# Pairing the pooling sums, one fp32 matmul per h, and 81 changed steps of the order, in a fused attention and maxout kernel

## The chip, the cores and the metric

The kernel runs on one core of a Trainium2 chip. The metric is the device time of one execution in microseconds (us), as a median of several runs. The engines are named as in the profile: PE (TensorE, matrix multiply), PEld (its weight loads), DVE (VectorE), ACT (ScalarE), POOL (GpSimd) and SP (SyncE, which here issues transfers). "L792" is line 792 of the kernel.

## The reference

There are two stages. The first is an attention through 32 inducing points, for four batch elements of 12544 tokens with 128 channels: the 32 points attend to all tokens and give h (32 x 128 for each batch element); then each token attends to the 32 rows of h. The second is a maxout layer on the result.

```python
# x: (4, 12544, 128), inducing: (32, 128); w1, w2: (128, 1024); w_out: (1024, 128)
def mab(q, kv):
    s = scale * (q @ kv.transpose(0, 2, 1))
    s = s - s.max(-1, keepdims=True)
    a = np.exp(s)
    a /= a.sum(-1, keepdims=True) + 1e-09
    return a @ kv
h = mab(I, x)                 # I: the inducing points, for each batch element
y = mab(x, h)                 # (4, 12544, 128)
h1 = y @ w1
h2 = y @ w2
out = np.maximum(h1, h2) @ w_out
```

"Pooling" below is the first `mab`: E = exp(scores), its sums, and h = (E x) / (sums of E).

## The kernel before

A batch element has 98 chunks of 128 tokens. The kernel writes max(h1, h2) as h1 + relu(h2 - h1), and folds h into the weights: a "phase" multiplies E2 (the second attention's exponentials, 32 rows for each of four blocks of tokens) by h (w2 - w1), the relu moves it from PSUM to SBUF on ACT (L973) or DVE (L976), and eight "final" matmuls per chunk (L792) multiply by w_out and add up. A "linear" part (L957 too, with the tile m) adds h1.

PE's array is used in three tilings. Final matmuls use it whole (128x128, "full"). A phase uses four row tiles of 32 rows, one for each block of tokens, side by side. Pooling and the staging of E2 use four column tiles of 32 columns ("col"). Every PE instruction's place in the program is fixed when the program is built, by a rule that keeps a rough clock `ck` of PE, ACT, DVE and the eight PSUM banks.

Pooling of the batch elements 1 to 3 runs beside the main loop of the element before. A unit is 16 chunks (NU = 6 units, and REST = 2 chunks left over). Scores of a unit go to one bank; ACT takes their exponential and, with it, the row sums (`accum_out`):

```python
        def pool_scores(b, u):
            if u == 0:
                st[b]["es"] = smp.tile([128, NU + 1], F32, name=f"es_{b}", tag="esu")
                nc.gpsimd.memset(st[b]["es"], 0.0)
            bi, ps = bank([128, 512])
            ck.wait(ck.bank[bi], "p1")
            for g in range(4):
                nc.tensor.matmul(
                    out=ps[32 * g : 32 * (g + 1), :],
                    lhsT=inducingT,
                    rhs=xT_tiles[b % 2][:, U * u + 4 * g : U * u + 4 * (g + 1), :],
                    start=True,
                    stop=True,
                    tile_position=(0, 32 * g),
                    skip_group_check=True,
                )
            end = ck.run(0.226, "col")
            eu = etp.tile([128, 512], F16, name=f"eu_{b}_{u}", tag="eu", bufs=NEU)
            nc.scalar.activation(
                out=eu, in_=ps, func=AF.Exp, scale=scale, accum_out=st[b]["es"][:, u : u + 1]
            )
            ck.bank[bi] = ck.on_act(end, 0.65)
            st[b]["eu", u] = eu, ck.bank[bi]

```

Each unit is turned by a transposing transfer, and then summed against x:

```python
        def pool_accum(b, u):
            bi, ps = bank([128, 512])
            ck.wait(ck.bank[bi], "p1")
            eT = st[b]["eT", u][0]
            st[b]["sum", u] = True
            last = u == NU - 1
            for j in range(4):
                for g in range(4):
                    nc.tensor.matmul(
                        out=ps[32 * g : 32 * (g + 1), 0:128],
                        lhsT=eT[:, j, 32 * g : 32 * (g + 1)],
                        rhs=xn_of(b, U * u + 4 * g + j),
                        start=(j == 0),
                        stop=(j == 3 and not (last and g < REST)),
                        tile_position=(0, 32 * g),
                        skip_group_check=True,
                    )
            if last:
                # ... (the REST chunks: E against x, and against a column of ones, into columns 0:128 and 128)
            end = ck.run(0.26, "col")
            if u == 0:
                st[b]["hacc"] = smp.tile([128, C], F32, name=f"hacc_{b}", tag="hacc")
                nc.vector.tensor_copy(out=st[b]["hacc"], in_=ps[:, 0:128])
            else:
                acc = st[b]["hacc"]
                nc.vector.tensor_add(out=acc, in0=ps[:, 0:128], in1=acc)
            ck.bank[bi] = ck.on_dve(end, 0.2)
            if last:
                es = st[b]["es"]
                nc.vector.tensor_copy(out=es[0 : 32 * REST, NU : NU + 1], in_=ps[0 : 32 * REST, 128:129])
                esr = smp.tile([128, 1], F32, name=f"esr_{b}", tag="esr")
                nc.vector.reduce_sum(out=esr, in_=es, axis=AX.X)
                st[b]["esr"] = esr
                ck.bank[bi] = st[b]["esrr"] = ck.on_dve(end, 0.2)
                if b + 1 < B:
                    for i in range(7):
                        load_x(b + 1, i, esr if i == 0 else None)
```

From these come h (`small_rep` spreads and inverts the sums, `small_h` transposes h and repeats it for the four row tiles):

```python
        def small_rep(b):
            bi, ps = bank([128, 512])
            ck.wait(ck.bank[bi], "p1")
            nc.tensor.matmul(out=ps[:, 0:1], lhsT=repd, rhs=st[b]["esr"], start=True, stop=True)
            end = ck.run(0.11)
            rec = smp.tile([128, 1], F32, name=f"rec_{b}", tag="rec")
            nc.vector.reciprocal(out=rec, in_=ps[:, 0:1])
            acc = st[b]["hacc"]
            nc.vector.tensor_scalar(out=acc, in0=acc, scalar1=rec, scalar2=None, op0=ALU.mult)
            ck.bank[bi] = st[b]["haccr"] = ck.on_dve(end, 0.4)

        def small_h(b):
            # ... (element 0 has its own way)
            bi, ps = bank([128, 512])
            ck.wait(ck.bank[bi], "p1")
            nc.tensor.matmul(out=ps[:, 0:128], lhsT=st[b]["hacc"], rhs=repd, start=True, stop=True)
            end = ck.run(0.25)
            nc.vector.tensor_copy(out=hT4.rearrange("c q m -> c (q m)"), in_=ps[:, 0:128])
            ck.bank[bi] = st[b]["hT4r"] = ck.on_dve(end, 0.2)
            st[b]["hT4"] = hT4.rearrange("c q m -> c (q m)")
```

The main loop: each pass places one thing. `column_work` places a staging or a pooling job; `phase` places a phase; `final_one` one final matmul. `tp` is when the phase's banks are free, `tf` when the next final's data are there.

```python
        def column_work(banks):
            # ... (False if too few banks; staging first, if due)
            jobs = [job for job in pending if job[0] in COL and ready(*job)]
            late = jobs and (chunks_done[0] >= due[jobs[0]] + 8 or jobs[0][1][1] == NU - 1)
            if jobs and (ck.mode == "col" or len(jobs) > 1 or late):
                pending.remove(jobs[0])
                f, a = jobs[0]
                f(*a)
                return True
            return False

        while state["g"] < len(groups) or held:
            side_work()
            if held and ck.mode == "full":
                linear_last(0.0)
            if ck.mode != "full" and column_work(1):
                continue
            if min(ck.bank) <= ck.pe + 0.1 and want_stage(1):
                stage(blocks[state["stage"]])
                state["stage"] += 1
                continue
            jobs = plan_phase()
            tp = INF
            tf = final_ready()
            useful = len(jobs) == 4 or jobs and (tf >= INF or state["stage"] == len(blocks) and lag() <= 48)
            if useful and len(jobs) > 0:
                fr = sorted(ck.bank)[len(jobs) - 1]
                tp = max([fr - 0.095] + [(a.blk.staged if kind == "L" else a.staged) for kind, q, a, u in jobs])
            early = 0.2 if ck.mode == "col" else 0.0
            if tp < INF and lag() <= 128 + LIMIT and (tp <= ck.pe + early or tp <= tf and tf > ck.pe):
                if column_work(len(jobs) + 1):
                    continue
                phase(jobs)
            elif tf < INF:
                keep_busy(tf)
                ck.wait(tf, "relu")
                final_one()
            elif tp < INF:
            # ...
```

The softmax here doesn't subtract the row's maximum and nothing guards it: scores larger than these inputs give would overflow.

## Time and profile before

| | |
|---|---|
| median time | 330.24 us (330.13 to 330.38, three runs) |
| span of the profiled execution | 328.5 us |
| TensorE clock granted | 1.00 throughout |
| mean transfer rate | 163 GB/s |

The parts of the pooling that the change touches have these rows among the groups kept apart by shape (line, engine, operation, output and inputs, shapes, count; then busy us, mean ns of one, and idle time before):

```profile
L357 PE MATMUL ps<-xn,eT 128*32 128x128 f16 x288 | 6.4, 220 | 0.1
L309 PE MATMUL ps<-xT,inducingT 128*32 128x512 f16 x72 | 6.3, 383 | 0.0
L385 DVE TENSOR_TENSOR hacc<-ps,hacc 128x128 f32<-128x128 f32 x15 | 4.3, 287 | 0.8
L430 PE MATMUL ps<-repd,hacc 128*128 128x128 f32 x6 | 1.3, 302 | 0.0
L401 PE MATMUL ps<-esr,repd 128*128 128x1 f32 x6 | 1.1, 246 | 0.5 <-DVE esr L391 0.3
L382 DVE COPY hacc<-ps 128x128 f32<-128x128 f32 x3 | 0.8, 281 | 0.0
L391 DVE TENSOR_REDUCE esr<-es 128x1 f32<-128x7 f32 x3 | 0.5, 160 | 0.3
```

A matmul of fp32 data appears as two matmuls: three of L401 and L430 in the program, six in the profile. Matmuls overlap in the pipeline, so one that lasts 220 ns can be followed by the next after much less: times between starts tell more than durations. The timeline merges neighbours of one line ("x13"), and its second column runs from the first one's start to the last one's end.

### The profile page before, as it was taken

To read this page: it belongs to the slowest core of one execution; us is meant where nothing else is said; L and a number is where in the kernel's file an instruction comes from. 1 tells how busy PE (TensorE), PEld (TensorE's weight loads), DVE (VectorE), ACT (ScalarE), POOL (GpSimd) and SP (SyncE) were. 2 spreads that over 40 slices of the span, in tenths; PEclk is the share of its full clock that TensorE was granted. 3 is DMA by queue.
4 is the path that set the end of the run, shared out by engine and by line. 5 is a ranking of instruction groups with operands and counts; after the bars stand their busy time and mean duration, and the time that the engine had idled before them with its cause. 6 is when DMAs were issued, how large, how long until landed. Compare 5 with 4: busy or idle time off the path is not lost.

```text
span 328.5 us, 12601 instructions
## 1 busy us (share of the span) xinstructions
PE 322.6 (98%) x5401; PEld 244.1 (74%) x5401; DVE 285.3 (87%) x532; ACT 280.7 (85%) x562; POOL 25.7 (8%) x54
## 2 busy tenths in 40 slices
PE   8999999999999999999999999999999999999996
PEld 3876777777777777777777777777777777778785
DVE  3359899999988999998989989988989989989873
ACT  3679899998789999988888999998968999999961
POOL 7351030000310000000040000000000000000000
PEclk9999999999999999999999999999999999999999
DMA  8999999964299999672479999983212312222233
GB/s 207 208 206 213 289 237 205 216 187 124 57 227 244 229 221 213 167 155 97 132 139 245 226 257 215 197 177 100 98 66 97 114 67 99 98 98 98 80 116 114
DMA packets 70823, 53.65 MB, mean 163 GB/s; under 512 B 52176, under 2 KB 55408, under 8 KB 70768
## 3 DMA queue, kind: packets, MB, share of 16 engines
q1 hardware_dynamic: 64656, 38.63, 47.4%
q0 software_dynamic: 6112, 14.22, 22.1%
q8 instruction: 42, 0.69, 0.9%
q14 instruction: 13, 0.11, 0.1%
HBM read 28.33 MB, written 25.69 MB: 164 GB/s over the span
## 4 chain that ended last, share of the span: by engine, by line
PE 96%; DVE 1%; issue 1%; ACT 0%; DVEq 0%; ACTq 0%
PE ps L792 60%; PE ps L957 22%; PE ps L582 3%; PE ps L232 2%; PE ps L357 1%; PE ps L309 1%; PE ps L648 1%; PE ps L248 1%; PE ps L280 1%; PE ps L622 1%; DVE relu L976 1%; PE ps L749 1%; PE ps L271 1%; PE ps L640 0%; PE ps L464 0%
## 5 line engine op out<-in xcount | busy, mean ns | idle before, releaser
L973 ACT ACTIVATE relu<-ps 128x512 f16<-128x512 f32 x463 | 244.6, 604 | 31.1 <-PE ps L957 24.1
L976 DVE TENSOR_SCALAR relu<-ps 128x512 f16<-128x512 f32 x321 | 205.8, 681 | 18.8 <-PE ps L957 17.9
L792 PE MATMUL ps<-woutp,relu 128*128 128x128 f16 x3136 | 218.1, 220 | 0.0
L792 PEld LDWEIGHTS <-relu 128*128 128x128 f16 x3136 | 177.3, 98 | 39.4 <-issue 28.3
L957 PE MATMUL ps<-e,hwd 32*128 32x512 f16 (+2 forms) x880 | 89.0, 360 | 0.0
L819 DVE TENSOR_TENSOR o<-ps,rp 128x512 f32<-128x512 f32 (+3 forms) x108 | 68.6, 635 | 5.7 <-PE ps L792 3.1
L957 PEld LDWEIGHTS <-hwd 32*128 32x128 f16 x880 | 25.0, 91 | 21.1 <-issue 0.8
L957 PE MATMUL ps<-m,e 32*128 32x128 f16 x381 | 38.8, 217 | 0.0
L957 PEld LDWEIGHTS <-e 32*128 32x128 f16 x381 | 21.4, 92 | 2.6
L165 POOL DMA_DIRECT2D xn<-in_x_dram x31 | 16.7, 551 | 8.4 <-DMA xn<-in_x_dram 4.4
L236 DVE COPY xT<-ps 128x512 f16<-128x512 f16 (+3 forms) x11 | 5.5, 504 | 8.1 <-PE ps L232 8.0
L594 ACT ACTIVATE e<-ps 128x512 f16<-128x512 f32 (+2 forms) x21 | 11.6, 572 | 0.0
L320 ACT ACTIVATE eu<-ps 128x512 f16<-128x512 f32 x18 | 10.8, 619 | 0.0
L582 PE MATMUL ps<-xT,hT 128*32 128x512 f16 (+3 forms) x114 | 10.4, 366 | 0.0
L164 POOL COPY pace<-esr 128x1 f32<-128x1 f32 x2 | 0.4, 183 | 116.6 <-DVE esr L391 116.6
L239 ACT COPY xT<-ps 128x768 f16<-128x768 f16 (+3 forms) x11 | 6.1, 557 | 3.0 <-PE ps L232 2.9
L232 PE MATMUL ps<-identity,xn 128*128 128x128 f16 x98 | 7.7, 224 | 0.1
L582 PEld LDWEIGHTS <-hT 128*32 128x32 f16 x114 | 2.9, 93 | 5.9 <-issue 5.2
L232 PEld LDWEIGHTS <-xn 128*128 128x128 f16 x98 | 5.9, 100 | 1.3 <-DVE xn L644 0.9
L257 ACT ACTIVATE et<-ps 128x448 f16<-128x448 f32 (+4 forms) x11 | 4.5, 413 | 2.6 <-PE ps L248 2.6
L632 DVE RECIPROCAL rp<-ps 128x16 f32<-128x16 f32 (+2 forms) x28 | 6.7, 239 | 0.0
L622 PE MATMUL ps<-ones_q,e 128*128 128x4 f16 x102 | 6.5, 165 | 0.0
(96 smaller groups left out, 117.5 us busy)
## 6 DMA issues: line engine op xcount, KB each, us to landing
out_dram<-o SPq DMA_DIRECT2D x90, 256.0 KB, 2.5
xn<-in_x_dram POOLq DMA_DIRECT2D x24, 448.0 KB, 11.9
out_dram<-o SPq DMA_DIRECT2D x10, 128.0 KB, 3.1
xn<-in_moe_w_dram POOLq DMA_DIRECT2D x4, 256.0 KB, 14.1
xn<-in_x_dram POOLq DMA_DIRECT2D x4, 224.0 KB, 10.2
xT<-xn SPq DMA_TRANSPOSE x42, 3.8
xf<-in_x_dram SPq DMA_DIRECT2D x1, 512.0 KB, 3.7
xf<-in_x_dram SPq DMA_DIRECT2D x1, 384.0 KB, 4.1
```

The costliest lines, as they stand in the source:

```text
L165: nc.gpsimd.dma_start(out=xn_at[b, i][:, 0:n, :], in_=xr[b, :, k0 : k0 + n, :])
L232: nc.tensor.transpose(ps[:, j, :], xn[:, g + j, :], identity16)
L320: nc.scalar.activation(out=eu, in_=ps, func=AF.Exp, scale=scale, accum_out=st[b]["es"][:, u : u + 1])
L582: nc.tensor.matmul(out=ps[32 * q : 32 * (q + 1), 128 * t : 128 * (t + n)], lhsT=hq, rhs=xT[:, c : c + n, :], start=True, stop=True, tile_p ...
L594: nc.scalar.activation(out=blk.e2[:, 0 : 128 * wd], in_=ps[:, 0 : 128 * wd], func=AF.Exp, scale=st[0]["rs"] if blk.b == 0 else scale,)
L622: nc.tensor.matmul(out=ps[:, 4 * t : 4 * t + 4], lhsT=blk.e2[:, 128 * t : 128 * (t + 1)], rhs=ones_q, start=True, stop=True,)
L632: nc.vector.reciprocal(out=blk.rp[:, 0:wd, :].rearrange("p t q -> p (t q)"), in_=ps[:, 0 : 4 * wd])
L792: nc.tensor.matmul(out=g.ps[:, 128 * c : 128 * (c + 1)], lhsT=g.blk.relu[q][:, 128 * (jb * w4 + t) : 128 * (jb * w4 + t + 1)], rhs=woutp[: ...
L819: nc.vector.tensor_mul(osb[:, 0:n, :], g.ps[:, 0 : n * C].rearrange("p (s c) -> p s c", s=n), rp)
L957: nc.tensor.matmul(**seq[i])
L973: nc.scalar.activation(out=dst, in_=src, func=AF.Relu)
L976: nc.vector.tensor_scalar(out=dst, in0=src, scalar1=0.0, scalar2=None, op0=ALU.max)
```

## The change

It has three parts. (1) The sums of two units (u = 1, 3, 5 with the unit before it) are gathered in one PSUM bank before DVE adds them to `hacc`. (2) The sums of E ride as a 129th column of `hacc`, so that one fp32 matmul spreads both h and its sums over the four row tiles; the scaled h becomes fp16 and is transposed by an fp16 transpose where it was multiplied in fp32. (3) A table `DEV` lists 81 passes of the main loop at which the order departs from its rule: 1 holds a phase back, 2 lets it start early, 3 skips column work, 4 lets a lone column job run. The 81 entries are 49, 7, 11 and 14 of these. The aim is fewer DVE instructions and fp32 matmuls in the pooling, and a better order on PE.

```diff
             if u == 0:
-                st[b]["es"] = smp.tile([128, NU + 1], F32, name=f"es_{b}", tag="esu")
-                nc.gpsimd.memset(st[b]["es"], 0.0)
+                st[b]["es"] = smp.tile([128, NU], F32, name=f"es_{b}", tag="esu")
 ...
         def pool_accum(b, u):
             bi, ps = bank([128, 512])
             ck.wait(ck.bank[bi], "p1")
-            eT = st[b]["eT", u][0]
-            st[b]["sum", u] = True
             last = u == NU - 1
-            for j in range(4):
-                for g in range(4):
-                    nc.tensor.matmul(
-                        out=ps[32 * g : 32 * (g + 1), 0:128],
-                        lhsT=eT[:, j, 32 * g : 32 * (g + 1)],
-                        rhs=xn_of(b, U * u + 4 * g + j),
-                        start=(j == 0),
-                        stop=(j == 3 and not (last and g < REST)),
-                        tile_position=(0, 32 * g),
-                        skip_group_check=True,
-                    )
+            if u == 1:
+                st[b]["hacc"] = smp.tile([128, C + 1], F32, name=f"hacc_{b}", tag="hacc")
+            acc = st[b]["hacc"]
+            if last:
+                nc.vector.reduce_sum(out=acc[:, C : C + 1], in_=st[b]["es"], axis=AX.X)
+                ck.on_dve(st[b]["eu", u][1], 0.1)
+            for v in (u - 1, u):
+                eT = st[b]["eT", v][0]
+                st[b]["sum", v] = True
+                for j in range(4):
+                    for g in range(4):
+                        nc.tensor.matmul(
+                            out=ps[32 * g : 32 * (g + 1), 0:128],
+                            lhsT=eT[:, j, 32 * g : 32 * (g + 1)],
+                            rhs=xn_of(b, U * v + 4 * g + j),
+                            start=(j == 0 and v < u),
+                            stop=(j == 3 and v == u and not (last and g < REST)),
+                            tile_position=(0, 32 * g),
+                            skip_group_check=True,
+                        )
             if last:
                 et = st[b]["et"][0]
-                for g in range(REST):
-                    for rhs, lo, n in ((xn_of(b, U * NU + g), 0, 128), (ones16[:, 0:1], 128, 1)):
+                for g in range(4):
+                    pairs = [(warm[:, 0:M], ones16[:, 0:1], 128, 1)]
+                    if g < REST:
+                        pairs = [
+                            (et[:, g, :], xn_of(b, U * NU + g), 0, 128),
+                            (et[:, g, :], ones16[:, 0:1], 128, 1),
+                        ]
+                    for lhsT, rhs, lo, n in pairs:
                         nc.tensor.matmul(
                             out=ps[32 * g : 32 * (g + 1), lo : lo + n],
-                            lhsT=et[:, g, :],
+                            lhsT=lhsT,
                             rhs=rhs,
                             start=False,
                             stop=True,
                             tile_position=(0, 32 * g),
                             skip_group_check=True,
                         )
-            end = ck.run(0.26, "col")
-            if u == 0:
-                st[b]["hacc"] = smp.tile([128, C], F32, name=f"hacc_{b}", tag="hacc")
-                nc.vector.tensor_copy(out=st[b]["hacc"], in_=ps[:, 0:128])
+            end = ck.run(0.58 if last else 0.49, "col")
+            n = C + 1 if last else C
+            if u == 1:
+                nc.vector.tensor_copy(out=acc[:, 0:n], in_=ps[:, 0:n])
             else:
-                acc = st[b]["hacc"]
-                nc.vector.tensor_add(out=acc, in0=ps[:, 0:128], in1=acc)
-            ck.bank[bi] = ck.on_dve(end, 0.2)
+                nc.vector.tensor_add(out=acc[:, 0:n], in0=ps[:, 0:n], in1=acc[:, 0:n])
+            ck.bank[bi] = ck.on_dve(end, 0.22)
             if last:
-                es = st[b]["es"]
-                nc.vector.tensor_copy(out=es[0 : 32 * REST, NU : NU + 1], in_=ps[0 : 32 * REST, 128:129])
-                esr = smp.tile([128, 1], F32, name=f"esr_{b}", tag="esr")
-                nc.vector.reduce_sum(out=esr, in_=es, axis=AX.X)
-                st[b]["esr"] = esr
-                ck.bank[bi] = st[b]["esrr"] = ck.on_dve(end, 0.2)
-                if b + 1 < B:
-                    for i in range(7):
-                        load_x(b + 1, i, esr if i == 0 else None)
+                st[b]["esrr"] = ck.bank[bi]
+            if last and b + 1 < B:
+                for i in range(7):
+                    load_x(b + 1, i, acc[:, C : C + 1] if i == 0 else None)
         def small_rep(b):
             bi, ps = bank([128, 512])
             ck.wait(ck.bank[bi], "p1")
-            nc.tensor.matmul(out=ps[:, 0:1], lhsT=repd, rhs=st[b]["esr"], start=True, stop=True)
-            end = ck.run(0.11)
+            nc.tensor.matmul(out=ps[:, 0 : C + 1], lhsT=repd, rhs=st[b]["hacc"], start=True, stop=True)
+            end = ck.run(0.28)
             rec = smp.tile([128, 1], F32, name=f"rec_{b}", tag="rec")
-            nc.vector.reciprocal(out=rec, in_=ps[:, 0:1])
-            acc = st[b]["hacc"]
-            nc.vector.tensor_scalar(out=acc, in0=acc, scalar1=rec, scalar2=None, op0=ALU.mult)
-            ck.bank[bi] = st[b]["haccr"] = ck.on_dve(end, 0.4)
+            nc.vector.reciprocal(out=rec, in_=ps[:, C : C + 1])
+            h4 = smp.tile([128, C], F16, name=f"h4_{b}", tag="h4")
+            nc.vector.tensor_scalar(out=h4, in0=ps[:, 0:C], scalar1=rec, scalar2=None, op0=ALU.mult)
+            st[b]["h4"] = h4
+            ck.bank[bi] = st[b]["haccr"] = ck.on_dve(end, 0.45)
         def small_h(b):
             hT4 = smp.tile([C, 4, M], F16, name=f"hT4_{b}", tag="hT4")
 ...
                 ready = ck.on_act(st[0]["end"], 0.2)
                 st[b]["hT4"] = hT4.rearrange("c q m -> c (q m)")
                 return es, ready
-            bi, ps = bank([128, 512])
+            bi, ps = bank([128, 128], F16)
             ck.wait(ck.bank[bi], "p1")
-            nc.tensor.matmul(out=ps[:, 0:128], lhsT=st[b]["hacc"], rhs=repd, start=True, stop=True)
-            end = ck.run(0.25)
+            nc.tensor.transpose(ps[:, 0:128], st[b]["h4"], identity16)
+            end = ck.run(0.056)
             nc.vector.tensor_copy(out=hT4.rearrange("c q m -> c (q m)"), in_=ps[:, 0:128])
             ck.bank[bi] = st[b]["hT4r"] = ck.on_dve(end, 0.2)
 ...
+        DEV = {
+            31: 1, 54: 1, 107: 2, 141: 1, 148: 1, 177: 4, 201: 1, 231: 1, 268: 1, 285: 1, 289: 1, 297: 2,
+            ... (81 entries in all)
+            1301: 4, 1349: 4, 1362: 3, 1363: 2, 1370: 4, 1379: 1, 1396: 2, 1435: 1, 1459: 1, 1469: 1, 1472:
+            3, 1519: 1, 1534: 1, 1536: 3, 1543: 4, 1572: 3, 1606: 1, 1617: 4, 1635: 1, 1654: 3, 1686: 1,
+            1701: 3, 1729: 1
+        }
 ...
-                at(base + int(acc), pool_accum, b, u)
+                if u % 2:
+                    at(base + int(acc), pool_accum, b, u)
 ...
-        def column_work(banks):
+        def column_work(banks, soon=False):
 ...
-            if jobs and (ck.mode == "col" or len(jobs) > 1 or late):
+            if jobs and (soon or ck.mode == "col" or len(jobs) > 1 or late):
                 pending.remove(jobs[0])
 ...
+        step = -1
         while state["g"] < len(groups) or held:
+            step += 1
+            how = DEV.get(step, 0)
             side_work()
             if held and ck.mode == "full":
                 linear_last(0.0)
-            if ck.mode != "full" and column_work(1):
+            if ck.mode != "full" and how != 3 and column_work(1):
                 continue
             if min(ck.bank) <= ck.pe + 0.1 and want_stage(1):
                 stage(blocks[state["stage"]])
                 fr = sorted(ck.bank)[len(jobs) - 1]
                 tp = max([fr - 0.095] + [(a.blk.staged if kind == "L" else a.staged) for kind, q, a, u in jobs])
             early = 0.2 if ck.mode == "col" else 0.0
-            if tp < INF and lag() <= 128 + LIMIT and (tp <= ck.pe + early or tp <= tf and tf > ck.pe):
-                if column_work(len(jobs) + 1):
+            now = tp <= ck.pe + early or tp <= tf and tf > ck.pe
+            if how == 1 and tf < INF:
+                now = False
+            if how == 2 and tp <= ck.pe + 0.2:
+                now = True
+            if tp < INF and lag() <= 128 + LIMIT and now:
+                if how != 3 and column_work(len(jobs) + 1, how == 4):
                     continue
                 phase(jobs)
```

## The prediction

> **What bounds the kernel now.** I read the page's busy shares first, then the costliest groups, then the busy times by stretch, then the timeline of TensorE. The busy shares and the groups:
>
> ```profile
> PE 322.6 (98%) x5401; PEld 244.1 (74%) x5401; DVE 285.3 (87%) x532; ACT 280.7 (85%) x562; POOL 25.7 (8%) x54
> ...
> L973 ACT ACTIVATE relu<-ps 128x512 f16<-128x512 f32 x463 | 244.6, 604 | 31.1 <-PE ps L957 24.1
> L976 DVE TENSOR_SCALAR relu<-ps 128x512 f16<-128x512 f32 x321 | 205.8, 681 | 18.8 <-PE ps L957 17.9
> L792 PE MATMUL ps<-woutp,relu 128*128 128x128 f16 x3136 | 218.1, 220 | 0.0
> ```
>
> Three engines are near their limit, so the question is which one is never waited for. The idle column answers: ScalarE (ACT) and VectorE (DVE) wait for TensorE's L957 matmuls (24.1 and 17.9 us), while L792 waits for nobody. By stretch, the long middle and the tail:
>
> ```profile
> 28.00:313.00 285.00, 284.46 (x4765) 214.50 (x4764) 264.24 (x480) 258.17 (x517) 11.71 (x23) 1.00 0.69 162
> 313.00:328.50 15.50, 12.24 (x227) 10.92 (x224) 8.12 (x16) 5.23 (x11) 0.00 (x0) 1.00 0.31 108
> ```
>
> Columns: length, then PE, weight loads, DVE, ACT, POOL, clock, DMA share, GB/s. In 285 us the PE is idle for 0.54 us; DVE has 20.8 us to spare, ACT 26.8. But a busy PE need not be a PE doing useful work, so I looked at starts, one to the next, in the PE timeline:
>
> ```profile
> 154.05 0.90 PE L792 MATMUL ps<-woutp,relu 128*128 128x128 f16 x13
> 154.88 0.40 PE L957 MATMUL ps<-e,hwd 32*128 32x512 f16 x4
> 155.21 0.23 PE L792 MATMUL ps<-woutp,relu 128*128 128x128 f16 x1
> ...
> 161.64 0.41 PE L357 MATMUL ps<-xn,eT 128*32 128x128 f16 x16
> 161.98 0.62 PE L792 MATMUL ps<-woutp,relu 128*128 128x128 f16 x8
> 162.53 0.39 PE L957 MATMUL ps<-e,hwd 32*128 32x512 f16 x3
> ```
>
> Thirteen final matmuls take 13 x 0.056 = 0.73 us, yet the next start is 0.83 after the first: 0.10 goes to the change from the whole array (128*128) to row tiles (32*128). The row phase streams 512 columns once, four tiles side by side (about 0.22), yet L792 starts 0.33 later: again some 0.10. I counted these changes over the whole PE timeline from 28 to 326 us: 219 row runs, 222 full runs, 35 column runs, 475 changes, so about 46 us of tiling changes (475 x 0.097). After a full run the next row phase starts a constant 0.152 us after the last full matmul started (median, 5th and 95th percentile within 0.004), so phases practically never wait for a bank. Apart from that I find, beyond streaming and changes, about 4 to 5 us of loss in this stretch, 2.5 of it in the small fp32 matmuls treated below.
>
> So the time is a sum: PE's matmuls plus its changes of tiling. A change helps only where it takes one of these away.
>
> **What the Trainium skill says.** "Perfetto Trace Analysis", section Identifying the Most-Contended Engine, warns that matmul busy time is no measure of distance to roofline because matmuls are pipelined; the trace agrees, as 46 us of the busy time are tiling changes, and weight loads are busy only 74%. "TensorEngine Tiling (Array Packing)", section Tiling Modes, says that a change of tiling mode (not of tile) drains TensorE; the trace gives it the size that the page lacks, 0.10 us. "TensorE: Matmul & The Clock Gate", section Back-to-back issue gap, gives N/2.4 + 2.5 ns, 55.8 ns for 128 columns; the trace's L792 median is 56. "VectorE: DVE Perf Modes", section Why PSUM operands drop a tier, says an fp32 operand in PSUM keeps DVE at its slowest rate; the trace agrees (a 128x512 product from PSUM 684 ns, 128x128 add 287), so each add removed is worth its full 0.29 us of DVE.
>
> **The change, part by part.**
>
> (1) *Two units' pooling sums in one bank.* Per batch element the six additions to hacc become three. Matmuls stay: 288 of L357, 16 per unit, about 0.23 us per unit. DVE loses 9 evictions, 9 x 0.287 = 2.6 us. On PE only visits to column mode can be saved. If every unit had its own visit, merging would give 9 x about 0.2. But the order already merges: L357 appears with 32 at 75.1, 48 at 80.5, 16 at 86.0 (first element: three visits); 32 at 139.1, 32 at 153.2, 16 at 161.6, 16 at 162.9 (second: four); 32 at 212.1, 224.6, 237.1 (third: three). Ten visits against nine: one is saved, 161.6 with 162.9. A visit of 16 costs 0.34 from start to L792, one of 32 costs 0.56, and a visit adds one change of 0.10: 2 x (0.34 + 0.10) - (0.56 + 0.10) = 0.2 us. Off the PE: -2.6 us of DVE; on it: -0.2 us.
>
> (2) *Sums of E as column 129, one fp32 matmul per h.* Before, each element had an fp32 matmul for the sums (L401) and one for h (L430), two passes each:
>
> ```profile
> 87.48 0.23 PE L792 MATMUL ps<-woutp,relu 128*128 128x128 f16 x1
> 87.78 0.35 PE L401 MATMUL ps<-esr,repd 128*128 128x1 f32 x2
> 88.00 0.22 PE L792 MATMUL ps<-woutp,relu 128*128 128x128 f16 x1
> ...
> 89.70 0.44 PE L430 MATMUL ps<-repd,hacc 128*128 128x128 f32 x2
> 89.98 1.06 PE L792 MATMUL ps<-woutp,relu 128*128 128x128 f16 x16
> ...
> 238.76 0.62 PE L792 MATMUL ps<-woutp,relu 128*128 128x128 f16 x8
> 239.69 0.35 PE L401 MATMUL ps<-esr,repd 128*128 128x1 f32 x2 [0.32 <-DVE esr L391]
> 239.91 0.55 PE L792 MATMUL ps<-woutp,relu 128*128 128x128 f16 x7
> ```
>
> L401 costs 0.22 plus the gap before it: 0.30 - 0.056 = 0.24 for the first element, about 0.25 for the second, 0.93 - 0.45 = 0.48 for the third, where the page names its releaser, the reduction that makes esr. Sum 3 x 0.22 + 0.97 = 1.63 us. L430 is 0.28 x 3 = 0.84. Together 2.47. After: one fp32 matmul of 129 columns, like L430 (0.28), an fp16 transpose (0.056 each, as L232: 14 in 0.78), and a gap that should shrink, because behind the last matmul DVE has one add of 129 columns (0.29) where it had add, copy and reduction (0.29 + 0.135 + 0.16, with gaps). The order also plans the matmul earlier by its own clock, so I keep a gap of 0.1. Per element 0.28 + 0.06 + 0.10 = 0.44; three are 1.3. Saving about 1.1 us. DVE also loses three small copies, 0.4 us. The zero-weight matmuls that give the other two groups their column are one column wide and beside others: nothing.
>
> (3) *81 listed steps.* One step is one pass of the loop: one final matmul, one phase, or one column job. 49 entries (value 1) hold a phase back for one step, 7 (value 2) let it start up to 0.2 us early, 11 (value 3) skip a column visit, 14 (value 4) run a column job that would have waited for company. The last entry, step 1729 of some 3400 (3136 finals plus phases and visits), lies near the middle, so the list touches about the first half. It can't change the number of finals, and the phases are full (four units, or three and one linear part), so row runs stay at about 220. Holding a phase back by 0.056 us moves work without removing any. What it can take away on PE: column visits merged with others (25 values concern these), at 0.1 us each, and small stalls, of which I find only about 1 us in the first half beside the fp32 ones. I put it at -0.3 us: four visits fewer, minus a little for new waits.
>
> Sum: -0.2 - 1.1 - 0.3 = -1.6 us; I shade this to -1.4, because the program's clock and the chip differ by tenths of a microsecond: 328.8 us.
>
> **The rivals.** *Evictions bind.* Phases come as soon as banks free: at the median phase, the third-last outstanding eviction ended only 0.1 us before. Then 3.0 us less DVE, shared by two engines, would give up to 1.5 us more, 327.3. Against it: PE has 0.54 us of idle time in 285, so an earlier phase only means later finals; the sum stays. *The list makes stalls.* It was made for the program's own clock, not the chip. Seven early starts of up to 0.2 us, and column jobs run ahead of a phase, could add 1 to 2 us, undoing the rest: 330 to 331. For it: the slack before phases is only 0.1 us; against it: in the kernel before nothing stalls although its order comes from the same clock. *The list merges many visits.* 35 column runs to about 25 would be -1.0 instead of -0.3: 328. *The fp32 matmul now waits longer,* since it reads hacc, which comes after the last add, where it read only sums: but those sums came behind the same add in DVE's order, so this costs nothing.
>
> **Range and chances.** The first rival and the third together end near 326.8, the second near 331. Eight in ten: 327.2 to 330.4. Faster by 2% would need 6.6 us, below 323.6; all that PE could lose (35 visits at 0.1, 2.5 of fp32, 2 of stalls) is about 8, and half of it must stay. Chance 0.03. Slower by 2% would need 6.6 us of new stalls where there are almost none: 0.03.
>
> **What would show it.** In the changed profile: DVE busy less by about 3 us with PE still at 98%; L792 still x3136 and about 220 row runs; the fp32 matmuls halved, with a wait under 0.2 us before each; column runs in the low thirties. I am wrong if row runs become far fewer (phases side by side, 0.2 us each), if final matmuls show idle time behind relu, or if phases start later than 0.152 us after the last full matmul's start in the first half.

## The result and the profile after

The changed kernel takes 327.82 us (median of six runs, 327.49 to 328.40) against 330.25 us before: a ratio of 0.9928, with a 95% interval of 0.9915 to 0.9940. That is 2.4 us, 0.7%, inside the predicted range; the prediction had 1.45 us.

The busy shares and the costliest groups of the changed kernel (L801 is the final matmul, L978 the phase, L994 and L997 the relu on ACT and DVE):

```profile
PE 320.8 (98%) x5404; PEld 243.0 (74%) x5404; DVE 282.3 (87%) x518; ACT 281.8 (86%) x564; POOL 25.4 (8%) x51
...
L994 ACT ACTIVATE relu<-ps 128x512 f16<-128x512 f32 x465 | 245.3, 605 | 25.3 <-PE ps L978 16.2
L997 DVE TENSOR_SCALAR relu<-ps 128x512 f16<-128x512 f32 x319 | 204.9, 682 | 19.8 <-PE ps L978 18.3
L801 PE MATMUL ps<-woutp,relu 128*128 128x128 f16 x3136 | 217.9, 220 | 0.1
```

DVE lost 3.0 us and 14 instructions; ACT and DVE still wait for PE's phases, and the finals' idle column still shows next to nothing (0.1 us). The busy times of the middle and of the tail (length, then PE, weight loads, DVE, ACT, POOL, clock, DMA share, GB/s):

```profile
28.00:310.70 282.70, 282.70 (x4769) 213.38 (x4768) 261.39 (x467) 259.46 (x519) 11.44 (x20) 1.00 0.71 163
310.70:326.20 15.50, 12.23 (x227) 10.91 (x223) 8.11 (x16) 5.22 (x11) 0.00 (x0) 1.00 0.31 107
```

The tail is unchanged; the middle is 2.3 us shorter, and the 0.54 us of visible PE idle time are gone. The step from pooling to h, in the PE timeline of the changed kernel:

```profile
164.30 0.23 PE L801 MATMUL ps<-woutp,relu 128*128 128x128 f16 x1
164.37 0.44 PE L409 MATMUL ps<-hacc,repd 128*128 128x129 f32 x2
164.65 1.00 PE L801 MATMUL ps<-woutp,relu 128*128 128x128 f16 x15
...
166.36 0.23 PE L439 MATMUL ps<-identity,h 128*128 128x128 f16 x1
166.43 0.50 PE L801 MATMUL ps<-woutp,relu 128*128 128x128 f16 x6
```

The one fp32 matmul starts 0.07 us after the final before it, so it has no gap, and holds PE for 0.28 us; the transpose takes 0.07. The other two elements have gaps of 0.17 and 0.01 us before it. Before, there were two fp32 matmuls of 0.22 and 0.28 us and gaps of 0.24 to 0.48.

Since a busy PE hides its losses, I split PE's time by the starts of its matmuls, from the first final on. A column visit is a run of matmuls on column tiles. A phase is given 0.327 us (its median), a column visit its streaming plus 0.11 us for the way out (its allowance); what goes beyond is called a wait. "h" is the fp32 matmuls with their gaps, and the transposes without theirs. The second number is the start of the run that holds the first final. Times in us, from the profiled execution of each kernel; the experiments in the lower rows follow below.

| kernel | span | first final's run at | h | column visits | their allowance | their waits | waits in phases | the rest |
|---|---|---|---|---|---|---|---|---|
| before | 328.49 | 25.89 | 2.46 | 35 | 16.79 | 0.89 | 1.74 | 280.72 |
| changed | 326.18 | 26.01 | 1.21 | 31 | 16.36 | 0.48 | 1.17 | 280.95 |
| no_list | 329.11 | 26.40 | 1.68 | 35 | 16.80 | 2.00 | 1.48 | 280.75 |
| column_only | 327.89 | 25.69 | 1.68 | 37 | 17.02 | 0.90 | 1.84 | 280.76 |
| pairs_only | 327.14 | 25.51 | 2.04 | 35 | 16.79 | 0.50 | 1.50 | 280.80 |
| first | 327.32 | 26.19 | 1.72 | 34 | 16.68 | 0.46 | 1.57 | 280.70 |
| late50 | 328.17 | 25.52 | 1.42 | 37 | 17.02 | 0.48 | 2.07 | 281.66 |
| no_list_later | 327.96 | 26.19 | 1.62 | 38 | 17.12 | 0.56 | 1.86 | 280.61 |
| copies_back | 326.24 | 25.66 | 1.21 | 31 | 16.36 | 0.47 | 1.59 | 280.95 |
| rule_only | 326.16 | 26.32 | 1.07 | 31 | 16.36 | 0.47 | 1.19 | 280.75 |

The last column, the finals with their tiling changes, the phases' 220 x 0.327 and the tail, is the same within 0.4 us in all rows but late50 (0.9 more). Apart from that, the differences between these orders lie in the small columns. From before to changed: h -1.25, allowance of the visits (four fewer) -0.43, their waits -0.41, phases' waits -0.57, first final +0.12, the rest +0.23; sum -2.31. In the rest are two new waits that the change brings: 0.11 us before the transpose at 166.36, which is released when DVE has scaled h, and 0.15 at the final that starts at 247.55, which is released by a relu. With the gaps of the transposes (0.12) h falls from 2.46 to 1.34, by 1.12.

A wait in a phase, as counted here, sits behind its first matmul. The longest before, 0.26 us, in the PE timeline of before:

```profile
246.50 0.38 PE L957 MATMUL ps<-e,hwd 32*128 32x512 f16 x1
246.60 0.21 PE L957 MATMUL ps<-m,e 32*128 32x128 f16 x1
246.76 0.39 PE L957 MATMUL ps<-e,hwd 32*128 32x128 f16 x2
```

The first starts the usual 0.15 us after the last final's start; the second comes 0.10 and the third 0.26 us behind it.

The first final's run starts anywhere between 25.5 and 26.4 us. The lists and rules act later, so this is taken for scatter of the opening; single spans can differ by 0.9 us through it, and the medians below are to be preferred. The kernel before, timed again beside each group of experiments, had medians of 330.17 to 330.45 us, so differences between kernels of different groups are good to some 0.3 us.

### The profile page after: what moved, and what is told of

It is laid out like the page before. It is cut to its first block, busy times and chain, and to the rows that moved or that the text cites. A ratio compares the mean times of both kernels' runs of the same rounds, so it can differ in the third digit from the quotient of the medians.

```text
span 326.2 us, 12587 instructions
## 1 busy us (share of the span) xinstructions
PE 320.8 (98%) x5404; PEld 243.0 (74%) x5404; DVE 282.3 (87%) x518; ACT 281.8 (86%) x564; POOL 25.4 (8%) x51
## 3 DMA queue, kind: packets, MB, share of 16 engines
HBM read 28.33 MB, written 25.69 MB: 166 GB/s over the span
## 4 chain that ended last, share of the span: by engine, by line
PE 98%; ACT 0%; issue 0%; DVE 0%; ACTq 0%
PE ps L801 61%; PE ps L978 23%; PE ps L591 3%; PE ps L232 2%; PE ps L364 1%; PE ps L308 1%; PE ps L657 1%; PE ps L248 1%; PE ps L280 1%; PE ps L631 1%; PE ps L649 1%; PE ps L758 1%; PE ps L271 1%; PE ps L473 0%; PE ps L409 0%
## 5 line engine op out<-in xcount | busy, mean ns | idle before, releaser
L994 ACT ACTIVATE relu<-ps 128x512 f16<-128x512 f32 x465 | 245.3, 605 | 25.3 <-PE ps L978 16.2
L997 DVE TENSOR_SCALAR relu<-ps 128x512 f16<-128x512 f32 x319 | 204.9, 682 | 19.8 <-PE ps L978 18.3
L801 PE MATMUL ps<-woutp,relu 128*128 128x128 f16 x3136 | 217.9, 220 | 0.1
L801 PEld LDWEIGHTS <-relu 128*128 128x128 f16 x3136 | 177.0, 98 | 40.7 <-issue 30.1
L978 PE MATMUL ps<-e,hwd 32*128 32x512 f16 (+2 forms) x880 | 88.7, 360 | 0.0
L978 PEld LDWEIGHTS <-hwd 32*128 32x128 f16 x880 | 24.6, 91 | 20.9 <-issue 0.8
L978 PE MATMUL ps<-m,e 32*128 32x128 f16 x381 | 38.8, 217 | 0.0
L978 PEld LDWEIGHTS <-e 32*128 32x128 f16 x381 | 21.3, 92 | 2.6
```

The lines of the kernel that those rows point to most:

```text
L801: nc.tensor.matmul(out=g.ps[:, 128 * c : 128 * (c + 1)], lhsT=g.blk.relu[q][:, 128 * (jb * w4 + t) : 128 * (jb * w4 + t + 1)], rhs=woutp[: ...
L978: nc.tensor.matmul(**seq[i])
L994: nc.scalar.activation(out=dst, in_=src, func=AF.Relu)
L997: nc.vector.tensor_scalar(out=dst, in0=src, scalar1=0.0, scalar2=None, op0=ALU.max)
```

## What the list holds

One thing can be read off the program. If the list is cut to four entries, at steps 107 (value 2), 1190, 1519 and 1729 (value 1), the instructions of all five engines stand in the same order as with 81, and so they do in the two traces (*four*, below). The other 77 fall on steps where they change nothing: a phase is held back that was not due, or column work is skipped where none was ready. None of the 25 entries of value 3 and 4 acts. Without entry 107 the other three fall on idle steps too.

## The experiments

**Each part alone.** Theory A is that of the prediction: the time is the sum of PE's matmuls, tiling changes and few waits. Theory B: the relief of VectorE is what counts. Theory C: the program's clock says nothing below a microsecond.

*no_list*: the changed kernel with an empty list.

```diff
-        DEV = {31: 1, 54: 1, 107: 2, ... }   # 81 entries
+        DEV = {}
```

> The changed kernel with an empty list: both changes of the pooling, the order by its rule. Theory A (the time is PE's matmuls plus its changes of tiling and the few waits): the fp32 matmuls are 1.1 us shorter, but the column runs are back at 35 in the stretch from 28 us on, as before the change, so 329.1 us, ratio 0.9965. Theory B (the 3 us taken from VectorE are what counts, the list is decoration): 328.0, as with the list.

Measured: 330.54 us, ratio to before 1.0007 (0.9995 to 1.0019). Both theories missed. The table says where: h is 0.8 us cheaper, where 1.1 was expected, and the waits in column visits are 1.1 us above before. It is one wait, in the PE timeline of no_list:

```profile
117.34 0.40 PE L591 MATMUL ps<-xT,hT 128*32 128x512 f16 x4
117.57 0.39 PE L308 MATMUL ps<-xT,inducingT 128*32 128x512 f16 x3
119.14 0.38 PE L308 MATMUL ps<-xT,inducingT 128*32 128x512 f16 x1 [1.19 <-DMA xT<-xn]
```

The first score job of element 2 starts at 117.57; three of its matmuls run, the fourth starts only at 119.14, released by a transposing transfer of tokens (xT<-xn). From start to start that is 1.57 us. The queue of SP, which issues these transfers in one line with the output stores, in the same run:

```profile
105.86 2.15 SPq L853 DMA_DIRECT2D out_dram<-o  x1
108.06 5.67 SPq L171 DMA_TRANSPOSE xT<-xn  x1
113.82 0.53 SPq L853 DMA_DIRECT2D out_dram<-o  x1
114.45 1.22 SPq L171 DMA_TRANSPOSE xT<-xn  x1
```

The transfer at 108.06 held the queue for 5.67 us where the usual one takes 1.28; the third, which the score job needs, was issued only at 114.45 and landed at 119.1. The 16 DMA engines were full then, but they were as full in the changed kernel. The stretch from 95 to 120 us in no_list and in the changed kernel (the last columns are the clock, the DMA share and GB/s):

```profile
95.00:120.00 25.00, 23.81 (x378) 17.14 (x378) 21.92 (x39) 23.33 (x45) 0.89 (x2) 1.00 1.10 228
95.00:120.00 25.00, 25.00 (x410) 18.78 (x404) 22.88 (x41) 22.79 (x45) 0.00 (x0) 1.00 1.14 230
```

Two times differ. The loads of the next element's tokens are let go by the last sums of element 1: at 87.9 us before, at 92.1 in no_list, at 89.8 in the changed kernel. The later they start, the longer one transfer holds the queue: at most 3.1 us where they start at 87.7 to 87.9 (before, column_only), 2.8 to 4.0 at 89.4 to 90.0 (changed, first, rule_only and rule_best among them), 5.7 to 6.8 at 91.5 to 93.6 (pairs_only, no_list, no_list_later, late50). And the score job itself starts at 127.4 before, at 117.6 in no_list, at 123.4 in the changed kernel, where the third transfer landed at 116.7. Later loads and earlier scores: so the rule, left alone with the new pooling, runs into a transfer that its clock takes for done. It is a near thing: in pairs_only a transfer holds the queue for 6.27 us too, but the third lands at 116.84, and the score job at 116.88 goes through without a wait.

*column_only* keeps the 129th column, the one fp32 matmul and the fp16 transpose, but sums each unit by itself; *pairs_only* keeps the pairing, but the old sums and the two fp32 matmuls. Both without a list.

```diff
# column_only, against no_list
-            for v in (u - 1, u):
+            for v in (u,):
 ...
-                if u % 2:
-                    at(base + int(acc), pool_accum, b, u)
+                at(base + int(acc), pool_accum, b, u)
# pairs_only, against no_list: the sums, small_rep and small_h as in the kernel before
+            nc.tensor.matmul(out=ps[:, 0:1], lhsT=repd, rhs=st[b]["esr"], start=True, stop=True)
 ...
+            nc.tensor.matmul(out=ps[:, 0:128], lhsT=st[b]["hacc"], rhs=repd, start=True, stop=True)
```

> Only the 129th column, one fp32 matmul and the fp16 transpose; every unit has its own bank and its own addition, as before; no list. Theory A: 329.2 us, the 1.1 us of fp32 and nothing else. Theory B: about half of the gain is missing, since VectorE has its nine additions back: 329.5 or more, and pairing alone brings the rest.

> Only the pairing: two units in one bank, nine additions fewer on VectorE; the sums, the two fp32 matmuls and the fp32 transpose as before; no list. Theory A: 330.0 us, since one column visit is saved at most. Theory B: 329.0, half of what nine additions of 0.287 us are worth when two engines share the evictions, or better.

Measured: column_only 329.91 us (0.9987, 0.9980 to 0.9994), pairs_only 329.31 us (0.9968, 0.9958 to 0.9978). The column saves 0.78 us at h and pays 0.23 for two more visits. Pairing saves no visit at all (35), but 0.39 us of waits inside visits, 0.24 in phases, and 0.42 at h. So the column is worth less alone than theory A said and pairing more, where theory B put it; but not yet by B's reason. The two gains, 0.4 and 1.0 us, add up to about what no_list would show without its wait of 1.57: 330.54 - 1.57 = 329.0. Both also shorten h, by 0.78 and 0.42, and together by 0.78 only, so the sum is no proof.

**VectorE's relief.** *copies_back* puts the load of the nine removed evictions back on DVE, with PE in the changed kernel's order.

```diff
             end = ck.run(0.58 if last else 0.49, "col")
+            junk = smp.tile([128, C], F16, name=f"junk_{b}_{u}", tag="junk", bufs=1)
+            nc.vector.tensor_copy(out=junk, in_=ps[:, 0:C])
```

> The changed kernel in the same order on PE, with the VectorE load of the nine removed evictions put back: at each of the nine pairs VectorE also copies 128 columns of the bank to a tile that nobody reads. Theory A (PE alone sets the end): 327.8 us as the changed kernel, at most 0.5 more where a phase just behind finds its bank 0.3 us later. Theory B (the relief of VectorE is what the pairing is worth): 1.3 to 2.6 us more, 329.1 to 330.4.

Measured: 328.45 us (0.9945, 0.9932 to 0.9958), 0.6 above the changed kernel's median; the two intervals overlap (changed: 0.9915 to 0.9940), and the traces say more. The table has 0.42 us more waits in phases, and they are two: 0.21 us at 140.0 and 0.18 at 215.1. The phase at 140, in the PE timeline of copies_back:

```profile
139.96 0.22 PE L980 MATMUL ps<-m,e 32*128 32x128 f16 x1
139.96 0.60 PE L980 MATMUL ps<-e,hwd 32*128 32x512 f16 x3
140.18 0.34 PE L980 MATMUL ps<-m,e 32*128 32x128 f16 x3
140.50 0.68 PE L803 MATMUL ps<-woutp,relu 128*128 128x128 f16 x9
```

and the same phase in the changed kernel:

```profile
140.31 0.23 PE L978 MATMUL ps<-m,e 32*128 32x128 f16 x1
140.32 0.39 PE L978 MATMUL ps<-e,hwd 32*128 32x512 f16 x3
140.38 0.33 PE L978 MATMUL ps<-m,e 32*128 32x128 f16 x3
140.64 0.57 PE L801 MATMUL ps<-woutp,relu 128*128 128x128 f16 x7
```

There the phase lasts 0.33 us. In copies_back it lasts 0.54: its first matmuls start at 139.96 and the rest at 140.18, while DVE does the extra copy (0.28 us, from 139.64) ahead of the copy into `hacc` (139.84 to 140.12) that frees the bank. Behind the other seven of the nine copies no phase waits longer. So 2.6 us of DVE work are worth about 0.5: not a rate, but the chance that a phase stands just behind. Theory A had allowed 0.5, theory B asked for 1.3 at least. In the changed kernel's order, then, VectorE's relief is worth some 0.5 us, about half of what pairs_only gained.

**The price of a change of tiling.** *excursions* adds 49 one-column matmuls of zero weights on a column tile between finals.

```diff
+            if finals[0] % 50 == 0 and 4 < state["mm"] < n * NJB:
+                nc.tensor.matmul(out=g.ps[0:32, 0:1], lhsT=warm[:, 0:32], rhs=warm[:, 0:1],
+                                 start=False, stop=False, tile_position=(0, 0), skip_group_check=True)
```

> The changed kernel in the same order, with 49 excursions into column tiling: after every fiftieth final matmul (where it stands inside a group) one matmul of a single column on a 32-column tile, with zero weights, added to the group's own bank. Theory A (each change of tiling drains PE and costs 0.097 us, and PE sets the end): 49 x (2 x 0.097 + 0.03) = 11 us more, 338.8. Rival (the 0.10 us seen in the timeline is latency that overlaps, or slack elsewhere takes it up): 1.5 to 3 us more.

Measured: 337.70 us (1.0219, 1.0206 to 1.0232), 9.9 us above the changed kernel, 0.20 us for each excursion. One of them in the PE timeline of this run:

```profile
47.21 0.84 PE L803 MATMUL ps<-woutp,relu 128*128 128x128 f16 x12
47.98 0.18 PE L815 MATMUL ps<-warm 128*32 128x1 f16 x1
48.09 0.28 PE L803 MATMUL ps<-woutp,relu 128*128 128x128 f16 x2
```

Twelve finals take 0.67 us; 0.10 passes before the excursion, and 0.11 from its start to the next final. Seven of the 49 stand just ahead of a phase and add one change instead of two; by the starts all 49 take 9.2 us of PE. Nothing elsewhere takes this up: the end moves by as much. So PE carries the end, and a visit between a phase and a final, which adds one change, costs 0.10 us beside its streaming.

**The list.** *late50* moves all its entries by 50 steps; *first* keeps only entry 107; *no_list_later* has no list and lets scores wait longer for their transfer.

```diff
# late50
+        DEV = {k + 50: v for k, v in DEV.items()}
# first
+        DEV = {107: 2}
# no_list_later, in the rule for scores
-                return d.get(("T", (U * a[1] + U - 1) // (P1 // 2)), INF) + 8.0 <= now
+                return d.get(("T", (U * a[1] + U - 1) // (P1 // 2)), INF) + 14.0 <= now
```

> The changed kernel with its list moved 50 steps later, so that the same number of departures falls on other steps. Theory A with the program's clock as guide: two column visits more than without any list, and waits before phases; 1.4 us above the run without a list, 330.5 us. Rival C (the clock of the program says nothing of the chip below a microsecond): within 0.3 us of the run without a list, or as fast as the changed kernel.

> The kernel without a list, but scores wait for 14 us instead of 8 after their tokens' transposing transfer was placed. In the run without a list PE stood 1.2 us (1.57 with what lies around it) at 117 us, at the second score job of element 2, for such a transfer. Theory A: that wait goes, 0.2 us of other losses come by the program's clock: 329.2 us. Rival (the wait hides a lack elsewhere and only moves): 330.5 as without a list.

> The changed kernel with the list cut to its entry at step 107 (a phase starts up to 0.2 us early). Of the 81 entries only those at steps 107, 1190, 1519 and 1729 alter the program at all; this is the first, without which the other three fall on steps where they do nothing. By the program's clock the first score job of element 2 then comes 18 us after its transfer was placed (12 us without a list, where PE stood waiting for it), and there is one column visit less. Theory A (waits and visits decide): the wait at 117 us is gone, 328.7 us, so that this one entry brings most of what the list brings, and the other three the last 0.9 us with three more visits saved. Rival (the list's gain lies in its many small shifts or in the other three): 330.0 or more.

Measured: late50 330.12 us (0.9999, 0.9990 to 1.0008), no_list_later 329.87 us (0.9989, 0.9981 to 0.9998), first 328.90 us (0.9952, 0.9937 to 0.9968).

In *first* the wait at 117 us is gone and its score job starts at 123.60 with all eight matmuls in 0.62 us. This one entry brings 1.64 us by the medians, and the table puts 1.54 of them into the waits of column visits. The other three entries bring the last 1.1: h -0.51 (its gap goes), visits -0.32 (three fewer), phases' waits -0.40, less the two new waits of 0.11 and 0.15 named above, which *first* does not have. The phases' waits are mostly one phase at the border of elements, in the PE timeline of *first*:

```profile
244.57 0.38 PE L978 MATMUL ps<-e,hwd 32*128 32x512 f16 x1
244.79 0.21 PE L978 MATMUL ps<-m,e 32*128 32x128 f16 x1
244.80 0.53 PE L978 MATMUL ps<-e,hwd 32*128 32x128 f16 x2
```

Its matmuls should start within some 0.06 us of one another; the second comes after 0.22, and the phase lasts 0.69 us from its start to the next column visit instead of 0.33. The changed kernel has no such phase there; the final at 247.55 waits in it instead.

In *no_list_later* the wait goes too, but only 0.67 us of the 1.57 come back: the later scores make three more visits (38) and 0.38 us more waits in phases. The expectation of 329.2 had counted on the clock, which had put all this at 0.2 us. (The job that waited in no_list is the first score job of element 2, not the second.) In *late50* the clock's verdict, 1.4 us worse than no list, fails as it stands: late50 is 0.4 us faster, since it too avoids the wait at 117. Against no_list without that wait (329.0) it is 1.1 us worse. The table has 0.22 of this in two more visits (37, as the clock had said), 0.59 in phases' waits, and 0.9 in the rest (waits at the borders of elements, such as 0.37 us before the phase at 97.0 and 0.28 before the final at 171.9), against 0.26 less at h. So the clock gave the direction in late50 and was 0.7 us short in no_list_later, and it knows nothing of a late transfer. Neither theory A nor theory C came out as written.

**Is there more in the order?** *rule_only* has no list, but five numbers of the rule are changed (transfers of elements 2 and 3 one chunk later, scores of element 1 later, 14 us for a transfer, column work only with a bank free within 0.095 us, and a lone job waits for company for 40 chunks). *searched12* has the result of a search over the rule's numbers with the clock as judge. *rule_best* repeats that search (one listed step is among its results), with the transfers left as in rule_only and no score job sooner than 14 us after its transfer. *four* is the list's acting four.

```diff
# rule_only, in part
-            t_first, t_step = (6, 2.2) if b == 1 else (-6, 3.4)
+            t_first, t_step = (6, 2.2) if b == 1 else (-5, 3.4)
-                    s, turn, acc = 25 + 5 * u, 45 + 1.5 * u, 55 + 2 * u
+                    s, turn, acc = 26 + 5.9 * u, 45 + 1.5 * u, 55 + 2 * u
# searched12, in part
+            t_first, t_step = (6, 2.2) if b == 1 else (-10, 1.75)
# rule_best, against rule_only, in part
+        DEV = {33: 2}
+                    s, turn, acc = 30.5 + 5.6 * u, 45 + 1.5 * u, 55 + 2 * u
+                    s = turn = 12.0 + 4.3 * u
+                    acc = s + 25.0
```

> No list; the same aim by five numbers of the rule: scores wait for 14 us after their transfer was placed, transfers are placed one chunk later, the scores of element 1 at 26 + 5.9 u instead of 25 + 5 u, column work waits for a bank free within 0.095 instead of 0.12 us, and a lone column job waits for company for 40 chunks instead of 8. The program's clock puts it 0.16 us below the changed kernel, with as few column visits and no score job sooner than 14.4 us after its transfer. Theory A: 327.7 us, level with the changed kernel. Rival (the listed steps have something that a rule can't give): above 328.5.

> An order found by a search over the numbers of the rule with the program's clock as judge: transfers of tokens placed 4 chunks earlier and 1.75 apart, scores as soon as they are ready (12 us after the transfer), lone jobs wait for company for 50 chunks, one listed step. The clock puts it 0.8 us below the changed kernel, but with three column visits more. Theory A (what counts on the chip are visits, at 0.2 us where they add two changes and 0.1 where one, and transfers that are late): no better than 327.8, perhaps 328.2, for the visits and for score jobs only 12 us behind their transfers. Rival (the clock is right to a few tenths): 327.0.

> The list cut to its four entries that act (steps 107, 1190, 1519, 1729); the instructions of every engine stand in the same order as in the changed kernel. It is here to measure how far one program differs between chips and calls, and as the changed kernel on the chip of the next run: 327.8 us, within 0.3. A difference beyond 0.5 would mean that medians of separate calls can't settle the smaller verdicts.

> The rule of the run rule_only, searched further with the transfers left where they are and no job sooner than 14 us after its transfer: scores of element 1 at 30.5 + 5.6 u, of the others at 12 + 4.3 u, sums 25 chunks after the scores, a lone job waits for company for 72 chunks, one listed step (33: 2). The program's clock puts it 0.2 us below rule_only and 0.36 below the changed kernel, at 34 column visits by its count against 33. Theory A (visits at 0.1 us and small waits): 327.6 to 328.0, not to be told from the changed kernel. Rival (there is still a microsecond in the order): 327.0 or less.

Measured: rule_only 328.18 us (0.9919, 0.9902 to 0.9935), four 327.88 us (0.9923, 0.9909 to 0.9936), rule_best 327.85 us (0.9924, 0.9911 to 0.9936). These three and the changed kernel can't be told apart; a rule gives what the list gives. No version beat the changed kernel.

searched12 took 351.96 us (1.0634, 1.0608 to 1.0659), which neither theory had. Its PE timeline:

```profile
120.64 0.23 PE L801 MATMUL ps<-woutp,relu 128*128 128x128 f16 x1
131.63 0.24 PE L330 MATMUL ps<-inducingT,xT 128*128 128x32 f16 x2 [10.75 <-DMA xT<-xn]
131.70 1.55 PE L801 MATMUL ps<-woutp,relu 128*128 128x128 f16 x13
```

The scores of the two left-over chunks (L330) need the last transposing transfer, which the clock takes for landed 6 us after it is placed. Placed early, these transfers stood in SP's queue one or two behind each output store, and the last was issued after 125.8 us. PE stood 10.9 us there and 7.2 us at the same place in element 3. Both stops also cost clock: the thirteen finals from 131.70 take 1.55 us where thirteen take 0.90 elsewhere, and the clock granted is 0.50:

```profile
131.60:135.00 3.40, 3.37 (x32) 2.74 (x33) 1.01 (x2) 0.51 (x2) 0.00 (x0) 0.50 0.42 153
```

It falls to one half at 123.3, 2.7 us into the stop, and is back at 137.0; after the second stop it stays at one half until 222.3. That is 11.1 us of work at half the clock, so by an estimate some 5.5 us more. With the 18.1 us of standing it makes up nearly all of the 24 us above the changed kernel. The search had found what its judge could not see.

## Why the prediction was right, step by step

- *PE's sum bounds the kernel, DVE and ACT do not.* Right. Excursions add 9.9 us for 9.2 of PE time, copies_back 0.6 us of 2.6.
- *h: -1.1 us.* Measured -1.25, with the gap that was kept at 0.10 us gone in two of three elements, and -1.12 with the gaps of the transposes, which the prediction had not thought of. But only 0.78 of the 1.25 belong to the column and its one fp32 matmul (column_only, no_list); the last 0.47 are the gap, which depends on the order.
- *Visits: one saved by pairing, four fewer by the list.* The profile has four fewer in all, 35 to 31, worth 0.43 us; pairing alone saved none.
- *Row runs at 220, L801 at 3136, DVE -3 us.* All as predicted.
- *Small stalls "minus a little for new waits".* This is the term that was mis-sized. The two terms beside h had -0.5 us together. The table has -1.41 for the visits with their waits and for the waits in phases, +0.35 for first final and rest: -1.06. The prediction had found 4 to 5 us of losses, 2.5 of them at h, and taken nearly all the others for fixed. The table has 2.63 us of waits before and 1.65 after: 0.98 went, and 0.27 of new ones came. The step that misled is "phases practically never wait for a bank". It looked at the first matmul of a phase alone, and that still starts 0.152 us after the last final; the waits sit behind it, inside the phase, as at 246.50 before. Pairing takes 0.39 us of the visits' waits and 0.24 of the phases' (pairs_only), the list another 0.31 in phases (no_list to changed).
- *The rival "evictions bind".* Wrong as a rate, but right in that DVE work at the wrong spot is paid for by the phase behind it.
- *The rival "the list makes stalls".* The reverse was so: the stall lay in the rule's own order under the new pooling, and the list avoids it. The prediction named the list as worth -0.3 us; against no_list it is worth 2.7, of which 1.5 undo a wait that appears only when the pooling is changed and the list left out. Total and parts thus agree less well than the total alone, and that is in part luck: a stall that was not foreseen was avoided by a list that was not known to avoid it.
- *The other two rivals.* The list merged visits to 31, not to 25. The fp32 matmul waits less than before (0.17, 0.01, 0.01 us against 0.24, 0.25, 0.48). By the prediction's own terms the first and third rival together end near 326.6, not 326.8.
- *55.8 ns for a final.* The Trainium skill, "TensorE: Matmul & The Clock Gate", section Back-to-back issue gap, gives N/2.4 + 2.5 ns for an isolated matmul, and about 81 ns at N = 128 for a stream of pairs of weight load and matmul. The finals are such a stream, and their median of 56 ns from start to start agrees with the former; the measurement decides.

What stays open: why pairing shortens the gap at h by 0.4 us without the column was not tried apart. What made the transfer at 108 us slow is not shown either: full DMA engines alone did not, and the loads' start goes with it in these traces, but no run moves the loads alone.

## What to carry to other kernels

Where the bounding engine never idles, compare two orders by what lies between its starts: count its changes of tiling, and sum what single stretches take beyond their usual length; busy shares show nothing of it. A list of order changes is worth testing by taking entries out: here 77 of 81 did nothing, and the first of the other four was worth most, because it avoids a late transfer. A schedule found on a model is only safe where the model has the queue that can be late: give such a queue a margin, or put it into the model.

## What the runs showed of the hardware

A change between whole-array and column tiling costs about 0.10 us each way, 0.20 us for a one-column matmul between two finals (excursions), and no other engine's slack takes it up. The Trainium skill, "TensorEngine Tiling (Array Packing)", section Tiling Modes, says that such a change drains TensorE; the runs give the price. A transposing transfer that usually held SP's queue for 1.28 us held it for up to 5.67 us, and took up to 10.4 us from issue to landing against a median of 4.0, in a stretch where the DMA engines were full (no_list); before, with engines as full, it was 3.08 and 9.4 us at most in that stretch. A stop of 11 us brought the granted clock of TensorE from 1.00 to 0.50 after 2.7 us, and the half clock outlasted the stop by 5.3 us (searched12).
